# Chunked attention beside a split-float32 FFN: another order for the pieces of attention

## The chip, the cores and the metric

The kernel runs on one core of a Trainium2 chip. The metric is the device time of one execution in microseconds (us). A difference of under 0.2% (about 2 us here) can't be told from no change.

## The reference

Attention works inside chunks of 64 tokens; its output, brought to 4608 rows of 512, goes through a two-layer FFN with a squared ReLU. The weights arrive as 64-bit floats, everything else as float32.

```python
scores = scale * np.matmul(q_c, k_c.transpose(0, 1, 2, 4, 3))     # chunks of 64 x 64
scores = scores - np.max(scores, axis=-1, keepdims=True)
attn = np.exp(scores)
attn = attn / (np.sum(attn, axis=-1, keepdims=True) + 1e-09)
out = np.matmul(attn, v_c)
x = np.ascontiguousarray(out.transpose(0, 2, 1, 3)).reshape(B * S, H * D)
h = x @ w_in                                  # 4608 x 512 by 512 x 2048
r = np.maximum(h, 0.0)
return ((r * r) @ w_out).astype(np.float32)   # by 2048 x 512
```

## The kernel before, in words

**Split floats.** Every product is taken in three parts: each operand is a rounded high part plus a low part (`fp32r`), and high by high, high by low and low by high are summed in PSUM. A low part is always `value - high`, so it needs the high part first.

**Blocks and steps.** The 4608 rows are 36 pairs of chunks (128 rows), in 9 blocks of 4 pairs. The FFN of a block is 16 steps; a step is 12 products of 128x512 into `h` (line 616) and 12 out of `g` (line 653), the second set two steps behind the first (`LAG = 2`). Between them ACT and DVE make `g`, `gh` and `gl`.

**Attention of a block runs during the FFN of the block before it.** Blocks 0 and 1 have their own code at the start. From block 2 on (pair 8 on) a pair is worked in two *units* of four heads; units 16 to 23 are block 2's, unit 71 is the last. A unit goes through this chain:

- `begin`/`stack`, once for a pair: q and k come by DMA into `ring` tiles, DVE transposes them (line 310), ACT and DVE split them into `qst` and `kst` (lines 315, 321, 327, 331).
- `scores`: four products `sc` on PE (line 357), called S16 to S71 below; ACT and DVE add the parts (370, 375), then maximum, subtraction, exponential, sums with reciprocal (379 to 393), and on POOL the division (`norm`, line 396).
- `turn`: DVE transposes the shares in 32x32 blocks into half 0 of the tile `turned` (`turn_p`, line 406); SP sends them to DRAM (`send_p`, line 410, tile `scr`) and fetches them back in four quarters into half 1 (`fetch_p`, line 417), which makes the transpose whole.
- `split_p`: ACT makes the high part of `pst` (`high_p`, line 423), DVE the low part (`low_p`, line 426).
- `values`: four products `xt` on PE (line 437), called X16 to X71 below. PE's order is fixed, so if `low_p` is late, PE stands at X and all FFN products behind it stand too. Then `x` is put together and split into `xh` and `xl` for the next block's FFN (447 to 465).

**What sets the order.** `program()` adds every piece to a `Plan` with an engine, a guessed cost and the tokens that it reads and writes. FFN pieces are added in order; the pieces of a unit are slipped in among them at fractions of the block (`SPOTS`, `LEAD`, `slot`, `spread`). `Plan.run` plays the list with its guesses (`greedy`, `to_the_right`, `to_the_left`) and issues each engine's instructions in order of the planned start. So a guess or a token doesn't make anything wait on the chip; it moves places in the five queues. On the chip each queue is worked strictly in that order, with semaphore waits on what an instruction really reads and overwrites. SP issues all transfers of this part from one queue: q and k (line 280), v (line 305), shares (410, 417) and results (670).

Of the kernel before, what the change touches and what calls it, by code (L numbers as in the profile page):

```python
# [22 lines left out]
def kernel(  # L23
# [661 lines left out]
    class Plan:  # L685
# [4 lines left out]
        HOP = {PE: 0.27, DVE: 0.07, ACT: 0.07, POOL: 0.1, SP: 0.1}  # L690
        LATENCY = 2.8
        RATE = 1.9e5
        END = 1e4

        def __init__(self):
            self.ops = []
            self.writer = {}
            self.readers = {}
            self.rank = 0
            self.follows = {}  # L700
            self.followed = {}
            self.last_load = None

        def add(self, engine, cost, fn, reads=(), writes=(), size=0):
# [12 lines left out]
            for t in reads:  # L717
                self.readers.setdefault(t, set()).add(n)
            self.ops.append((engine, cost, fn, before - {n}, size, self.rank))
            if engine == SP and self.rank is not None:  # L720
# [8 lines left out]
        def greedy(self):  # L729
# [6 lines left out]
            for n in reversed(range(len(ops))):  # L736
                engine, cost, _, _, size, rank = ops[n]
                if size:
                    cost += size / self.RATE + self.LATENCY
# [10 lines left out]
            while open_:  # L750
# [7 lines left out]
                t, _, n = best  # L758
                engine, cost, fn, _, size, _ = ops[n]
                end = free[engine] = t + cost  # L760
                if size:
                    queue = max(queue, end) + size / self.RATE
                    end = queue + self.LATENCY
                if loads and loads[-1] == n:
# [34 lines left out]
        def to_the_right(self, start, after):  # L799
            ops = self.ops  # L800
            last = max(start[n] + ops[n][1] for n in start)
            busy = self.busy()
            right = {}
            for n in sorted(start, key=lambda n: (start[n], n), reverse=True):
                engine, cost, _, _, size, _ = ops[n]
                t = min((right[x] - self.hop(n, x) for x in after[n]), default=last)
                if size:
                    t = self.lately(busy, "queue", t - self.LATENCY, size / self.RATE)
                if n in self.followed:
                    t = min(t, right[self.followed[n]])  # L810
                right[n] = self.lately(busy, engine, t, cost)
            return right

        def to_the_left(self, right):
# [3 lines left out]
            for n in sorted(right, key=lambda n: (right[n], n)):  # L818
                engine, cost, _, before, size, _ = ops[n]
                t = max((end[x] + self.hop(x, n) for x in before), default=0.0)  # L820
                if n in self.follows:
                    t = max(t, start[self.follows[n]] + ops[self.follows[n]][1])
                start[n] = t = self.early(busy, engine, t, cost)
                end[n] = t + cost
                if size:
                    end[n] = self.early(busy, "queue", t + cost, size / self.RATE) + size / self.RATE + self.LATENCY
            return start
# [23 lines left out]
    def program():  # L851
# [230 lines left out]
        ]  # L1082
        spread(ops, spots)
        for b in range(1, len(blocks)):
            later(p, b)
# [6 lines left out]

    SPOTS = (0.0, 0.12, 0.62)
    KB = 1024
# [3 lines left out]
    def later(p, b):  # L1098
# [56 lines left out]
        def fetch_v(pair):  # L1155
            if pair < NPAIR:
                un = unit[NQ * pair]
                for c in range(2):
                    for r in range(2):
                        add(SP, 0.55, lambda c=c, r=r: un.load_v(c, r), ["late"], [("vraw", c, r)], size=128 * KB)  # L1160

# [29 lines left out]
        def scores(un):  # L1191
# [19 lines left out]
            add(DVE, 0.8, un.sums, every, [z])  # L1211
            add(POOL, 0.65, un.norm, [z], every)

        quarters = [(half, b) for half in range(2) for b in range(IH)]

        def turn(un):
            e = ("le", un.u % 2)
            every = [e] + [(*e, part, c) for part in range(2) for c in range(2)]
            scr = ("scr", un.u % 2)
            add(DVE, HALF, un.turn_p, every, [("ob", 0)])  # L1220
            add(SP, 0.5, un.send_p, [("ob", 0)], [scr], size=128 * KB)
            for x in quarters:
                add(SP, 0.5, lambda x=x: un.fetch_p(*x), [scr], [("ob", 1, x), *([("ob", 1)] if un.u == NQ * NN else [])], size=64 * KB)

# [23 lines left out]
        def slot(t):  # L1248
            r = []
            for at_, stages in zip(SPOTS, (((0, split_p),), ((1, scores), (1, turn), (2, begin)), ((0, values), (1, split_v)))):  # L1250
                r.append((at_, [lambda st=st, un=unit[t + on]: st(un) for on, st in stages if t + on < NU]))
# [23 lines left out]
        spots = []  # L1275
        start = 0.0
        if b == 1:
            u = NQ * NN
            spots.append((LEAD, [lambda: scores(unit[u]), lambda: turn(unit[u]), lambda: split_v(unit[u]), lambda: begin(unit[u + 1])]))
            start = LEAD + (1 - LEAD) * (1 - SPOTS[1]) / (NQ * blocks[2] + 1 - SPOTS[1])  # L1280
        if not last:
            n = NQ * blocks[b + 1]
            for i in range(n):
                spots += [(start + (1 - start) * (i + x) / n, fs) for x, fs in slot(NQ * first_pair[b + 1] + i)]
        spread(ops, spots)
# [49 lines left out]
```

## Time and profile before

| | |
|---|---|
| median of 3 runs | 934.14 us (933.08 to 934.48) |
| the profiled execution | 933.78 us, span 932.0 us |
| busy share: PE, DVE, ACT, POOL | 96%, 70%, 68%, 24% |
| granted TensorE clock, mean | 0.991 |

The span runs from the first to the last instruction that the profiler saw; the rest of the execution lies around it. A busy share is a mean over stages: what matters here are the moments in which PE stands, and what ended each of them.

### The profile page before, as it was taken

Reading aid. Unit: us, or ns where it says so; the run is one execution under the profiler, and the core shown is the slowest. Engines: PE = TensorE matmul, PEld = TensorE weight load, DVE = VectorE, ACT = ScalarE, POOL = GpSimd, SP = SyncE. Lnnn points to the kernel's source line nnn. Section 1 sums busy time; section 2 is a strip of 40 time slices with the busy share of each in tenths; the row PEclk is TensorE's granted clock in tenths of the full one; section 3 lists DMA queues with packets and bytes.
Section 4 is the critical chain, followed back from the end, with each engine's and each line's share of the span. In section 5 each row is a group of like instructions: output and inputs, shape, how many; then the busy total and the mean of one; then the engine's idle time right before and its main releaser. Section 6 shows DMA issues by size and latency. Waiting matters only on the chain.

```text
span 932.0 us, 14557 instructions
## 1 busy us (share of the span) xinstructions
PE 897.5 (96%) x4290; PEld 747.2 (80%) x4290; DVE 656.2 (70%) x1374; ACT 631.0 (68%) x1388; POOL 227.7 (24%) x354
## 2 busy tenths in 40 slices
PE   8899998689899999999999999999999999999998
PEld 7788887567778888887878888878788888888886
DVE  4999976476787787777777777767777887742111
ACT  5898857376777777767777777767777776743223
POOL 3000002133233232433242323323323333210000
PEclk9999999799999999999999999999999999999999
DMA  9896115223343334433343334333433353201001
GB/s 212 241 334 163 46 26 133 54 68 78 84 121 74 80 80 100 105 80 80 93 102 75 77 76 127 79 77 75 112 75 72 75 130 72 57 18 46 1 1 45
DMA packets 262991, 84.87 MB, mean 91 GB/s; under 512 B 212224, under 2 KB 256256, under 8 KB 262912
## 3 DMA queue, kind: packets, MB, share of 16 engines
q1 hardware_dynamic: 260800, 83.42, 36.8%
q10 hardware_dynamic: 2112, 0.52, 0.3%
q8 instruction: 34, 0.56, 0.3%
q14 instruction: 45, 0.37, 0.1%
HBM read 67.11 MB, written 16.78 MB: 90 GB/s over the span
## 4 chain that ended last, share of the span: by engine, by line
PE 77%; DVE 8%; ACT 6%; DMA 3%; issue 3%; SPq 2%; POOL 1%; DVEq 0%; POOLq 0%; ACTq 0%
PE o L653 35%; PE h L616 34%; PE xt L437 3%; PE sc L357 2%; DVE e L375 1%; PE sc L528 1%; POOL e L396 1%; DVE pst L426 1%; DMA raw<-in_moe_w_out_dram 1%; DMA v_raw<-in_v_dram 1%; ACT x L447 1%; ACT kst L327 1%; DVE x L454 1%; ACT g L627 1%; ACT e L370 1%
## 5 line engine op out<-in xcount | busy, mean ns | idle before, releaser
L616 PE MATMUL h<-xh,w 128*128 128x512 f32 x1152 | 398.2, 392 | 0.0
L653 PE MATMUL o<-w,gh 128*128 128x512 f32 x1152 | 358.7, 393 | 0.0
L653 PEld LDWEIGHTS o<-w,gh 128*128 128x128 f32 x1152 | 216.7, 189 | 46.2 <-DVE outl L665 0.2
L616 PEld LDWEIGHTS h<-xh,w 128*128 128x128 f32 x1152 | 217.5, 189 | 41.7 <-DVE w L210 0.4
L616 PE MATMUL h<-xl,w 128*128 128x512 f32 x576 | 225.8, 392 | 0.2 <-DVE xl L592 0.2
L653 PE MATMUL o<-w,gl 128*128 128x512 f32 x576 | 225.3, 391 | 0.0
L643 DVE TENSOR_TENSOR gl<-g,gh 128x512 fp32r<-128x512 f32 x144 | 103.3, 717 | 92.1 <-ACT gh L640 89.8
L627 ACT ACTIVATE g<-h 128x512 f32<-128x512 f32 x144 | 86.2, 599 | 98.6 <-DVE gl L643 46.2
L347 POOL TENSOR_TENSOR vs<-v_raw,vs 64x128 fp32r<-64x128 f32 x224 | 117.3, 524 | 127.8 <-ACT vs L342 116.9
L640 ACT CAST gh<-g 128x512 fp32r<-128x512 f32 x144 | 89.4, 621 | 71.3 <-DVE g L631 33.6
L653 PEld LDWEIGHTS o<-w,gl 128*128 128x128 f32 x576 | 108.9, 189 | 23.5
L616 PEld LDWEIGHTS h<-xl,w 128*128 128x128 f32 x576 | 108.9, 189 | 18.7 <-DVE xl L592 0.5
L375 DVE TENSOR_TENSOR e<-sc,e 64x128 f32<-64x128 f32 x224 | 64.7, 289 | 57.7 <-ACT e L370 54.8
L465 POOL TENSOR_TENSOR xl<-x,xh 128x256 fp32r<-128x256 f32 x56 | 45.4, 811 | 219.8 <-ACT xh L462 175.9
L396 POOL TENSOR_TENSOR e<-e,z 128x256 f32<-128x256 f32 x56 | 54.8, 979 | 139.2 <-DVE z L393 134.5
L454 DVE TENSOR_TENSOR x<-xt,x 64x128 f32<-64x128 f32 x224 | 64.7, 289 | 12.8 <-ACT x L447 7.5
L370 ACT COPY e<-sc 64x128 f32<-64x128 f32 x224 | 58.2, 260 | 21.1 <-PE sc L357 17.9
L327 ACT CAST kst<-ring 64x512 fp32r<-64x512 f32 x112 | 69.3, 619 | 3.8 <-DVE ring L310 1.5
L447 ACT COPY x<-xt 64x128 f32<-64x128 f32 x224 | 58.0, 259 | 9.3 <-PE xt L437 6.5
L631 DVE TENSOR_TENSOR g<-g 128x512 f32<-128x512 f32 x64 | 47.3, 739 | 23.4 <-ACT g L627 23.0
L437 PE MATMUL xt<-pst,vs 128*128 128x256 f32 x224 | 37.6, 291 | 23.9 <-DVE pst L426 23.7
L437 PEld LDWEIGHTS xt<-pst,vs 128*128 128x128 f32 x224 | 33.0, 191 | 33.9 <-issue 23.8
(71 smaller groups left out, 880.8 us busy)
## 6 DMA issues: line engine op xcount, KB each, us to landing
v_raw<-in_v_dram SPq DMA_DIRECT2D x112, 128.0 KB, 3.2
turned<-scr SPq DMA_DIRECT2D x224, 64.0 KB, 2.0
raw<-in_moe_w_in_dram SPq DMA_DIRECT2D x16, 512.0 KB, 6.8
raw<-in_moe_w_out_dram SPq DMA_DIRECT2D x16, 512.0 KB, 7.7
scr<-turned SPq DMA_DIRECT2D x56, 128.0 KB, 1.7
ring<-in_q_dram SPq DMA_DIRECT2D x216, 32.0 KB, 2.1
ring<-in_k_dram SPq DMA_DIRECT2D x216, 32.0 KB, 2.2
out_dram<-outh SPq DMA_DIRECT2D x18, 256.0 KB, 2.2
```

Source lines behind the costliest of these rows:

```text
L327: nc.scalar.copy(late["k"][other[c][half], 0, c], pairs[self.pair]["t", 1][own])
L347: nc.gpsimd.tensor_tensor(self.v[:, c][dst], self.raw_v(c)[dst], self.v.bitcast(F32)[:, c][dst], op=ALU.subtract)
L370: nc.scalar.copy(self.e[r, 2 * part:2 * part + 2], self.done[part][r, :, 1, c])
L375: nc.vector.tensor_tensor(e, self.done[part][r, :, 0, c], e, op=ALU.add)
L437: nc.tensor.matmul(self.xt[hp][:, c].rearrange("p w b a i -> p (w b a i)"), self.v[:, c, hp].rearrange("p a d -> p (a d)"), late["p"][:, : ...
L447: nc.scalar.copy(self.x[r, hp].rearrange("p c (b i) -> p c b i", b=IH), self.xt[hp][r, :, 1, :, h2])
L454: nc.vector.tensor_tensor(x, self.xt[hp][r, :, 0, :, h2], x, op=ALU.add)
L616: nc.tensor.matmul(self.h[:, :self.n], a[:, c], bb[:, c % HP, :self.n], start=c == 0 and i == 0, stop=c == NCC - 1 and i == 2,)
L627: nc.scalar.activation(self.g, self.h[:, :self.n], AF.Relu)
L640: nc.scalar.copy(self.gh[:, :self.n], self.g)
L643: nc.vector.tensor_tensor(self.gl[:, :self.n], self.g, self.gh.bitcast(F32)[:, :self.n], op=ALU.subtract)
L653: nc.tensor.matmul(acc[b, j], a[:, j * P:(j + 1) * P], bb, start=f == 0 and i == 0, stop=f == NF - 1 and i == 2,)
```

## The change

Eleven numbers and two tokens of the planner's input change; no instruction is added, removed or made larger.

```diff
-        LATENCY = 2.8
...
+            self.latency = 2.8
...
         spread(ops, spots)
+        p.latency = 1.5
         for b in range(1, len(blocks)):
             later(p, b)
...
-    SPOTS = (0.0, 0.12, 0.62)
+    SPOTS = (0.0, 0.1, 0.66)
+    SPOTS1 = (0.0, 0.15, 0.8)
...
-                        add(SP, 0.55, lambda c=c, r=r: un.load_v(c, r), ["late"], [("vraw", c, r)], size=128 * KB)
+                        add(SP, 0.65, lambda c=c, r=r: un.load_v(c, r), ["late"], [("vraw", c, r)], size=128 * KB)
...
-            add(POOL, 0.65, un.norm, [z], every)
+            add(POOL, 1.0, un.norm, [z], every)
...
-            add(DVE, HALF, un.turn_p, every, [("ob", 0)])
-            add(SP, 0.5, un.send_p, [("ob", 0)], [scr], size=128 * KB)
+            add(DVE, HALF, un.turn_p, [*every, ("pst", 1)], [("ob", 0)])
+            add(SP, 0.4, un.send_p, [("ob", 0)], [scr, *([("ob", 1)] if un.u == NQ * NN else [])], size=128 * KB)
             for x in quarters:
-                add(SP, 0.5, lambda x=x: un.fetch_p(*x), [scr], [("ob", 1, x), *([("ob", 1)] if un.u == NQ * NN else [])], size=64 * KB)
+                add(SP, 0.5, lambda x=x: un.fetch_p(*x), [scr], [("ob", 1, x)], size=64 * KB)
...
-            for at_, stages in zip(SPOTS, (((0, split_p),), ((1, scores), (1, turn), (2, begin)), ((0, values), (1, split_v)))):
+            for at_, stages in zip(SPOTS1 if b == 1 else SPOTS, (((0, split_p),), ((1, scores), (1, turn), (2, begin)), ((0, values), (1, split_v)))):
...
-        start = 0.0
+        start, end = 0.0, 1.0
         if b == 1:
...
-            start = LEAD + (1 - LEAD) * (1 - SPOTS[1]) / (NQ * blocks[2] + 1 - SPOTS[1])
+            start, end = 0.2, 0.975
...
-                spots += [(start + (1 - start) * (i + x) / n, fs) for x, fs in slot(NQ * first_pair[b + 1] + i)]
+                spots += [(start + (end - start) * (i + x) / n, fs) for x, fs in slot(NQ * first_pair[b + 1] + i)]
```

`LATENCY`, what the plan allows from the end of a transfer's issue and bytes to its landing, is now kept with each operation. In unit 16 (`un.u == NQ * NN`) each of the four fetches wrote the token `("ob", 1)`, so the plan put each behind the landing of the one before; now only the send writes it. `turn_p` reads `("pst", 1)`, the token that `low_p` of the unit before writes. `start` for block 2 goes from 0.207 to 0.2 of block 1's FFN and `end` from 1 to 0.975.

The next two lists are SP's queue from the send of unit 16's shares on (`scr_1545` before, `scr_1567` after), before and after:

```order
L410 DMA scr_1545<-turned 128x256
L670 DMA out_dram<-outl_1466 128x512
L305 DMA v_raw_0_1562<-in_v_dram 64x8x64 x2
L305 DMA v_raw_1_1576<-in_v_dram 64x8x64 x2
L417 DMA turned<-scr_1545 32x4x128
L280 DMA ring_1326<-in_q_dram 32x8x32 x6
L417 DMA turned<-scr_1545 32x4x128
L280 DMA ring_1326<-in_q_dram 32x8x32 x2
L410 DMA scr_1647<-turned 128x256
L280 DMA ring_1324<-in_k_dram 32x8x32 x2
L417 DMA turned<-scr_1545 32x4x128
L280 DMA ring_1324<-in_k_dram 32x8x32 x6
```

```order
L670 DMA out_dram<-outl_1466 128x512 x2
L305 DMA v_raw_0_1540<-in_v_dram 64x8x64 x2
L410 DMA scr_1567<-turned 128x256
L280 DMA ring_1326<-in_q_dram 32x8x32 x4
L417 DMA turned<-scr_1567 32x4x128 x4
L280 DMA ring_1326<-in_q_dram 32x8x32 x4
L280 DMA ring_1324<-in_k_dram 32x8x32 x5
L410 DMA scr_1674<-turned 128x256
L280 DMA ring_1324<-in_k_dram 32x8x32 x3
```

Before, five more issues (four of v) stand between the send and the first fetch, and 16 loads and the next send between the first fetch and the fourth, which follows the last row. After, the four fetches stand together behind four loads.

DVE in the same place: from the maximum of unit 17 (`e_1595` before, `e_1592` after) to `pst`, which is the low part of unit 16:

```order
L379 TENSOR_REDUCE m_1614<-e_1595 128x4
L382 TENSOR_TENSOR e_1595<-e_1595,m_1614 128x256
L391 TENSOR_REDUCE z_1630<-e_1595 128x4
L392 TENSOR_SCALAR z_1630<-z_1630 128x4
L393 RECIPROCAL z_1630<-z_1630 128x4
L321 TENSOR_TENSOR qst<-ring_1324,qst 64x8x64
L406 STREAM_TRANSPOSE turned<-e_1595 128x256
L321 TENSOR_TENSOR qst<-ring_1324,qst 64x8x64
L331 TENSOR_TENSOR kst<-ring_1325,kst 64x512 x2
L643 TENSOR_TENSOR gl_3_1653<-g_3_1583,gh_3_1652 128x512
L310 STREAM_TRANSPOSE ring_1325<-ring_1326 128x512
L310 STREAM_TRANSPOSE ring_1326<-ring_1324 128x512
```

```order
L379 TENSOR_REDUCE m_1611<-e_1592 128x4
L382 TENSOR_TENSOR e_1592<-e_1592,m_1611 128x256
L321 TENSOR_TENSOR qst<-ring_1324,qst 64x8x64 x2
L391 TENSOR_REDUCE z_1638<-e_1592 128x4
L392 TENSOR_SCALAR z_1638<-z_1638 128x4
L393 RECIPROCAL z_1638<-z_1638 128x4
L331 TENSOR_TENSOR kst<-ring_1325,kst 64x512
L426 TENSOR_TENSOR pst<-turned,pst 128x512
L331 TENSOR_TENSOR kst<-ring_1325,kst 64x512
L406 STREAM_TRANSPOSE turned<-e_1592 128x256
```

Before, `pst` is the row behind the last one shown, behind the turn of unit 17 and two transposes of later q and k; after, it is ahead of the turn and of those transposes.

The same engine in the middle of the kernel, from the subtraction of unit 38 (`e_4439`, `e_4434`) on; `pst` is the low part of unit 37:

```order
L382 TENSOR_TENSOR e_4439<-e_4439,m_4456 128x256
L391 TENSOR_REDUCE z_4466<-e_4439 128x4
L392 TENSOR_SCALAR z_4466<-z_4466 128x4
L393 RECIPROCAL z_4466<-z_4466 128x4
L643 TENSOR_TENSOR gl_9_4426<-g_9_4414,gh_9_4425 128x512
L406 STREAM_TRANSPOSE turned<-e_4439 128x256
L426 TENSOR_TENSOR pst<-turned,pst 128x512
```

```order
L382 TENSOR_TENSOR e_4434<-e_4434,m_4457 128x256
L426 TENSOR_TENSOR pst<-turned,pst 128x512
L391 TENSOR_REDUCE z_4471<-e_4434 128x4
L392 TENSOR_SCALAR z_4471<-z_4471 128x4
L393 RECIPROCAL z_4471<-z_4471 128x4
L631 TENSOR_TENSOR g_10_4469<-g_10_4469 128x512
L406 STREAM_TRANSPOSE turned<-e_4434 128x256
```

The low part goes from behind the turn to ahead of the sums. On the whole, `pst` stands behind the next unit's turn for 10 of the 56 units before (16, 19, 21, 23, 25, 37, 41, 53, 57, 67) and for none after.

On PE only the places of S and X among the FFN's products move. Counted in the order: from S to X of one unit there are 54 to 63 products in units 16 to 23 before and 60 to 63 after, and 72 before and 75 after from unit 25 on. X16 stands behind the 465th product before and the 468th after, X25 behind the 825th in both.

## Rows read from the trace of the kernel before

**Rows 1.** The page: its head; one stretch by engine (busy us, instructions, clock, DMA).

```profile
span 932.0 us, 14557 instructions
...
292.00:840.00 548.00, 543.28 (x2549) 452.76 (x2548) 414.27 (x945) 394.62 (x948) 171.14 (x266) 1.00 0.36 83
```

**Rows 2.** Waits from 146 to 292 us and from 292 to 832 us: total, times, longest.

```profile
PE xt L437 <- DVE pst L426: 19.1, 7, 10.3
...
PE xt L437 <- DVE pst L426: 4.6, 5, 1.0
```

**Rows 3.** Timeline of PE: X16, S18, X18, X25, two S a unit apart, X37, X70.

```profile
170.79 1.20 PE L437 MATMUL xt<-pst,vs 128*128 128x256 f32 x4 [10.29 <-DVE pst L426]
177.22 0.64 PE L357 MATMUL sc<-kst,qst 128*128 128x256 f32 x4
194.36 0.71 PE L437 MATMUL xt<-pst,vs 128*128 128x256 f32 x4 [1.81 <-DVE pst L426]
278.55 0.71 PE L437 MATMUL xt<-pst,vs 128*128 128x256 f32 x4 [1.58 <-DVE pst L426]
296.45 0.64 PE L357 MATMUL sc<-kst,qst 128*128 128x256 f32 x4
308.33 0.64 PE L357 MATMUL sc<-kst,qst 128*128 128x256 f32 x4
422.76 0.71 PE L437 MATMUL xt<-pst,vs 128*128 128x256 f32 x4 [1.01 <-DVE pst L426]
820.07 0.64 PE L437 MATMUL xt<-pst,vs 128*128 128x256 f32 x4
```

**Rows 4.** Timelines of DVE and ACT: turn 16; high and low 16; low 17, turn 18.

```profile
151.61 0.45 DVE L406 STREAM_TRANSPOSE turned<-e 128x256 f32<-128x256 f32 x1
169.31 0.62 ACT L423 CAST pst<-turned 128x512 fp32r<-128x512 f32 x1 [6.15 <-DMA turned<-scr]
169.96 0.69 DVE L426 TENSOR_TENSOR pst<-turned,pst 128x512 fp32r<-128x512 f32 x1
181.64 0.69 DVE L426 TENSOR_TENSOR pst<-turned,pst 128x512 fp32r<-128x512 f32 x1
182.84 0.45 DVE L406 STREAM_TRANSPOSE turned<-e 128x256 f32<-128x256 f32 x1 [0.51 <-POOL e L396]
```

**Rows 5.** Timeline of SP's queue: unit 16's send, first and fourth fetch; unit 18's.

```profile
152.08 0.33 SPq L410 DMA_DIRECT2D scr<-turned  x1
157.20 0.57 SPq L417 DMA_DIRECT2D turned<-scr  x1
167.14 0.45 SPq L417 DMA_DIRECT2D turned<-scr  x1
183.31 0.34 SPq L410 DMA_DIRECT2D scr<-turned  x1
185.09 1.74 SPq L417 DMA_DIRECT2D turned<-scr  x4
```

**Rows 6.** DMA issues (count, KB, median us to landing); landing of the shares from 190 to 203 us.

```profile
v_raw<-in_v_dram SPq DMA_DIRECT2D x112, 128.0 KB, 3.2
turned<-scr SPq DMA_DIRECT2D x224, 64.0 KB, 2.0
...
DMA to landing us min/median/max: 1.7/3.2/3.5
```

**Rows 7.** Stretches by engine, as in Rows 1: just behind X16, X18 and X19.

```profile
170.70:174.90 4.20, 4.11 (x12) 3.51 (x13) 1.85 (x5) 2.54 (x8) 0.63 (x1) 0.54 0.45 96
194.90:198.30 3.40, 3.40 (x11) 2.64 (x10) 3.23 (x7) 2.52 (x8) 1.41 (x2) 0.53 0.38 80
208.70:212.10 3.40, 3.40 (x10) 2.69 (x9) 1.85 (x5) 2.38 (x7) 1.37 (x3) 0.51 0.40 83
```

**Rows 8.** Timeline of DVE at X37: turn 38, low part of 37.

```profile
421.60 0.45 DVE L406 STREAM_TRANSPOSE turned<-e 128x256 f32<-128x256 f32 x1 [0.51 <-POOL e L396]
421.97 0.65 DVE L426 TENSOR_TENSOR pst<-turned,pst 128x512 fp32r<-128x512 f32 x1
```

More of the change, by code (lines that the diff above doesn't have):

```diff
@@ L718, in add @@
                 self.readers.setdefault(t, set()).add(n)
-            self.ops.append((engine, cost, fn, before - {n}, size, self.rank))
+            self.ops.append((engine, cost, fn, before - {n}, size, self.rank, self.latency))
             if engine == SP and self.rank is not None:
@@ L736, in greedy @@
             for n in reversed(range(len(ops))):
-                engine, cost, _, _, size, rank = ops[n]
+                engine, cost, _, _, size, rank, latency = ops[n]
                 if size:
-                    cost += size / self.RATE + self.LATENCY
+                    cost += size / self.RATE + latency
                 due[n] = min((due[x] - self.hop(n, x) for x in after[n]), default=self.END) - cost
@@ L758, in greedy @@
                 t, _, n = best
-                engine, cost, fn, _, size, _ = ops[n]
+                engine, cost, fn, _, size, _, latency = ops[n]
                 end = free[engine] = t + cost
@@ L762, in greedy @@
                     queue = max(queue, end) + size / self.RATE
-                    end = queue + self.LATENCY
+                    end = queue + latency
                 if loads and loads[-1] == n:
@@ L804, in to_the_right @@
             for n in sorted(start, key=lambda n: (start[n], n), reverse=True):
-                engine, cost, _, _, size, _ = ops[n]
+                engine, cost, _, _, size, _, latency = ops[n]
                 t = min((right[x] - self.hop(n, x) for x in after[n]), default=last)
                 if size:
-                    t = self.lately(busy, "queue", t - self.LATENCY, size / self.RATE)
+                    t = self.lately(busy, "queue", t - latency, size / self.RATE)
                 if n in self.followed:
@@ L818, in to_the_left @@
             for n in sorted(right, key=lambda n: (right[n], n)):
-                engine, cost, _, before, size, _ = ops[n]
+                engine, cost, _, before, size, _, latency = ops[n]
                 t = max((end[x] + self.hop(x, n) for x in before), default=0.0)
@@ L825, in to_the_left @@
                 if size:
-                    end[n] = self.early(busy, "queue", t + cost, size / self.RATE) + size / self.RATE + self.LATENCY
+                    end[n] = self.early(busy, "queue", t + cost, size / self.RATE) + size / self.RATE + latency
             return start
```

## The prediction

> **What bounds the kernel now.** I read the busy time by stretch first: from 292 to 840 us PE is busy for 543.28 of 548 us at the full clock [rows 1]. The middle is PE's own work; only its idle moments and its slow stretches can be won. The list of waits says what ends the idle moments: the products `xt` (X) wait for the low part of `pst`, seven times from 146 to 292 us, 19.1 us with one of 10.3, and five times later, 4.6 us [rows 2]. No other wait of PE there is worth a term.
>
> The timeline of PE gives the cost with what hangs on the waits. In the middle one unit lasts 308.33 - 296.45 = 11.88 us [rows 3]: 48 products at some 0.227 us, S and X at about 0.5 each. From X25 (278.55) to X70 (820.07) stand 45 units, 534.6 us at that pace; they took 541.5 [rows 3]. So **the middle has 6.9 us** to give. From X16 (170.79) to X25 there are 360 products and nine S and nine X, about 81.6 + 9.2 = 90.8 us; they took 107.8 [rows 3]. So there are **17.0 us here**, and 10.3 in the wait before X16.
>
> Part of the 17.0 is the clock. In three stretches, behind X16, X18 and X19, the granted clock was 0.54, 0.53 and 0.51 of full speed, which is the lower level of 1.2 GHz, each after PE had stood [rows 7]. They last 4.2, 3.4 and 3.4 us, so they cost 1.9 + 1.6 + 1.7 = 5.2 us. The six labelled waits behind X16 are 19.1 - 10.3 = 8.8 us [rows 2]. The other 3.0 us are smaller delays around the waits that have no label.
>
> **The change, part by part.** Nothing is added or taken away, so every cost is one of place.
>
> *The fetches of unit 16.* Its shares are turned at 151.61 [rows 4] and sent at 152.08; the first fetch is issued at 157.20, the fourth at 167.14 [rows 5]. ACT stood 6.15 us for it, the high part started at 169.31, the low part at 169.96 [rows 4], X16 at 170.79. In the new queue the four fetches stand together behind four loads. Unit 18 shows what that is worth: turn 182.84 [rows 4], send 183.31, four fetches from 185.09 in 1.74 us [rows 5], landing 2.0 us after an issue [rows 6]: the data are there about 188.4, **5.6 us after the turn starts**. Four loads fit into the time in which the first fetch waits for the send anyway (183.31 to 185.09). In the new order DVE copies one more result and transposes q ahead of unit 16's parts, and squares and transposes k before the turn: four pieces of about 0.7 us, some of them in a wait that was there before. I take turn 16 at 153.2 instead of 151.61 and the data at 158.8 instead of 169.3. Then they are not last.
>
> What is late next is DVE itself, whose list up to the low part of 16 now has S17's parts, the maximum, two low parts of q, the sums and one low part of k. Without q and k this took from S18 at 177.22 to 181.64 + 0.69 = 182.33, 5.1 us [rows 3, 4]. Three pieces of about 0.69 are added, of which I let 0.5 fill the wait for the exponential: 6.7 us. S17 stands 36 products behind S16 (which is where it was, 146.4), at 155.0; the low part ends at 161.7 and X16 starts at 161.8 to 162. PE arrives 24 products after S17, at 160.9. So about 1.1 us of the wait of 10.29 stays. X16 comes at 162.0, with three more products behind it: **8.8 us earlier**, and 0.7 more by the three products. Bounds: if everything but the fetch is hidden, 9.9; if the turn comes 4 us later than I take it, as it would if the v loads that now stand ahead of the send wait for POOL, 5.
>
> *Low part ahead of the turn.* At X37 DVE first waits 0.51 us for POOL, turns unit 38's shares (421.60), and only then makes the low part of 37 at 421.97 [rows 8]; PE waits 1.01 us for it and starts at 422.76 [rows 3]. The lists show this at X16, 19, 21, 23, 25, 37, 41, 53, 57 and 67; the timeline of PE has a wait at each, and only X18 and X20 wait without it. In the new order no turn stands there. From unit 24 on the low part is ahead even of the sums (about 0.8 us) in most units and X stands three products (0.7 us) later. So the middle should run at its pace: **-6.7 us** of the 6.9. Can the moved turn be late instead? It closes a loop: turn, data after 5.6 us, high part 0.62, low part 0.69 [rows 4], sums 0.8, 1.2 us from their end (181.64, where the next row starts) to the turn (182.84) [rows 4], and one square of 0.7: 9.7 us, against 11.88 for a unit. It is hidden with 2.2 us to spare. (The 0.8 and 0.7 are the plan's figures; its 0.69 for a low part is what the row shows.)
>
> *Block 2.* Here a unit has only 37 products on average (X16 to X23, 468 to 729 in the order): 8.5 + 1.0 = 9.5 us, against the same loop of 9.7. There is no cover left, so I expect waits of a few tenths to 1 us where q and k are split in between: about 1.0 at X18, 0.3 each at X21 and X22, and 1.0 in all at scores that now follow X by 12 products (3.3 us) instead of 18. That is 2.5 us instead of 8.8 + 3.0. None is as long as those of 1.8 us and more after which the clock fell, and waits of 1.01 us passed without a fall [rows 3], so I take the 5.2 us as won. Together 17.0 - 2.5 = **-14.5 us**. Bounds: all of 17.0, if nothing waits; 3.5, if the waits stay and the clock still falls once for 1.7.
>
> The other edits (guesses for v, send and `norm`, the spots) act through these orders; the lists up to S16 are the same but for neighbours.
>
> **Sum.** Against the profiled execution's own 933.8 us (0.4 below the median of 934.14): 933.8 - 8.8 - 0.7 - 14.5 - 6.7 = 903.1. I give one microsecond back for delays that I don't see: **904 us**.
>
> **Rivals.** *A: the fetches land later.* Shares that followed six loads of k landed after 3.2 us in the middle and 3.5 at most, not 2.0 [rows 6]. In block 2 that makes the loop 9.7 + 1.3 = 11.0 us against 9.5: seven units wait 1.5 us, 10.5 instead of the 2.5, and the clock falls once for 1.7. 904 + 8 + 1.7 = **914 us**. For it: in the new order each block of fetches follows up to four loads, and in unit 18 a load of v of 128 KB, which takes 3.2 us [rows 6], where before the fetches came first. Against it: over all 224 fetches the median is 2.0, though by the order most followed loads too. The Trainium skill (*DMA: Bandwidth & Descriptors*, section *Queues, rings and completion order*) speaks for A: a transfer's completion signal is ordered behind every earlier write of the same DMA engine, so fetches behind loads land no sooner than these. By that rule the new neighbours delay every unit and A is the result; the trace bears it out for one place of those that I looked at.
>
> *B: half of X16's wait stays*, because the send stands behind loads of v that wait for POOL: 5 us more and a slow stretch of 1.9: **911 us**. Against it: POOL is idle for most of that time.
>
> *C: slower.* The turn now waits for the low part, the low part for the data, the data for the turn before. If this loop lasted longer than a unit of the middle, every unit would be late. Its point is 11.88 us, 2.2 above the 9.7. To eat the 30 us won, 47 units must lose 0.64 each, a loop of 12.5; with fetches at the 3.5 us of the slowest row it is 11.2. At 13 us the time is 904 + 47 x 1.1 = **956 us**.
>
> *D: the order changes nothing*, since X16 hangs on something else in the same queue: 930 to 934. The 6.15 us that ACT stood for the fetch speak against it.
>
> **How the numbers follow.** Forecast 0.62, with its own range of 900.5 to 909 (899.3 would be all the bounds won, 933.8 - 9.9 - 0.7 - 17.0 - 6.9); A 0.2; B 0.12; C 0.04; D 0.02. The range from 900.5 to 914 leaves out C, D and the worse half of A. 0.2% is 1.9 us: faster 0.95, same 0.01, slower 0.04.
>
> **What would show it.** X16 at 161 to 163 us with a wait near 1 us; fetches of unit 16 in one row of four; X25 near 254 us; no wait of X for `pst` behind 260 us and 11.88 us from S to S; a full clock behind X18 and X19. Wrong if X18 to X23 wait 1.5 us each (A), if the send of unit 16 comes behind 155 us (B), or if S to S is above 12 us in the middle (C).

## The result and the profile after

The changed kernel takes 903.98 us (median of four runs, 903.73 to 904.32) beside 934.31 us of the kernel before on the same chip (933.08 to 935.25): a ratio of 0.9676, 95% interval 0.966 to 0.9693, that is 30 us less. The forecast was 904. Its profiled execution is the one of 903.73 us. The size is right nearly term by term; what the terms come from is not as I said, and that is the larger part of what follows.

From the page and from single views of the kernel after: the head of the page, the middle by engine (columns as in [rows 1]), and what X waited for from 146 to 292 us. Behind 292 us that view has no line for X any more.

```profile
span 901.9 us, 14559 instructions
...
292.00:840.00 548.00, 548.00 (x2572) 459.13 (x2572) 402.58 (x914) 393.88 (x923) 163.74 (x254) 1.00 0.35 82
...
PE xt L437 <- DVE pst L426: 3.2, 5, 1.1
```

In the timeline of PE of the kernel after these rows are X16, S18, X18, X21, S25, S26, X25 and X70, to be read beside [rows 3]:

```profile
162.13 0.71 PE L437 MATMUL xt<-pst,vs 128*128 128x256 f32 x4 [0.88 <-DVE pst L426]
165.43 0.64 PE L357 MATMUL sc<-kst,qst 128*128 128x256 f32 x4
182.46 0.71 PE L437 MATMUL xt<-pst,vs 128*128 128x256 f32 x4 [1.08 <-DVE pst L426]
212.14 0.71 PE L437 MATMUL xt<-pst,vs 128*128 128x256 f32 x4 [0.89 <-DVE pst L426]
237.32 0.64 PE L357 MATMUL sc<-kst,qst 128*128 128x256 f32 x4
249.20 0.64 PE L357 MATMUL sc<-kst,qst 128*128 128x256 f32 x4
255.82 0.64 PE L437 MATMUL xt<-pst,vs 128*128 128x256 f32 x4
790.41 0.64 PE L437 MATMUL xt<-pst,vs 128*128 128x256 f32 x4
```

And these are the turn of unit 16 on DVE, its send and its four fetches in SP's queue and its low part on DVE, beside [rows 4, 5]:

```profile
152.99 0.41 DVE L406 STREAM_TRANSPOSE turned<-e 128x256 f32<-128x256 f32 x1
153.43 0.33 SPq L410 DMA_DIRECT2D scr<-turned  x1
156.46 1.73 SPq L417 DMA_DIRECT2D turned<-scr  x4
161.31 0.68 DVE L426 TENSOR_TENSOR pst<-turned,pst 128x512 fp32r<-128x512 f32 x1
```

The reader is to see three things. PE is busy for all 548.00 us of the middle, where it was for 543.28. X16 starts at 162.13 instead of 170.79. And no wait of X is longer than 1.1 us; from 146 to 840 us the granted clock is full in every stretch.

| term | forecast | measured, from the rows |
| --- | --- | --- |
| to X16 | -8.8 | 162.13 - 170.79 = -8.66 |
| X16 to X25 | -0.7 - 14.5 = -15.2 | (255.82 - 162.13) - (278.55 - 170.79) = -14.07 |
| X25 to X70 | -6.7 | (790.41 - 255.82) - (820.07 - 278.55) = -6.93 |
| the rest | +1 given back | 903.73 - 933.78 + 29.66 = -0.39 |

### The profile page after: what moved, and what is told of

It reads as the page before. It is cut to its first block, busy times and chain, and to the rows that moved or that the text cites. A ratio compares the mean times of both kernels' runs of the same rounds, so it can differ in the third digit from the quotient of the medians.

```text
span 901.9 us, 14559 instructions
## 1 busy us (share of the span) xinstructions
PE 890.3 (99%) x4290; PEld 746.1 (83%) x4290; DVE 657.2 (73%) x1374; ACT 638.3 (71%) x1388; POOL 228.7 (25%) x354
## 4 chain that ended last, share of the span: by engine, by line
PE 93%; DVE 3%; ACT 1%; issue 1%; SPq 1%; DMA 1%; POOL 0%; DVEq 0%; POOLq 0%; ACTq 0%
PE h L616 42%; PE o L653 42%; PE xt L437 3%; PE sc L357 3%; PE sc L528 1%; PE xt L579 1%; DVE e L375 1%; PE warm_ps L866 0%; DVE qst L321 0%; PE k L504 0%; DVE pst L426 0%; PE q L504 0%; DMA qk_raw<-in_q_dram 0%; DVE e L382 0%; ACT e L370 0%
## 5 line engine op out<-in xcount | busy, mean ns | idle before, releaser
L347 POOL TENSOR_TENSOR vs<-v_raw,vs 64x128 fp32r<-64x128 f32 x224 | 121.2, 541 | 155.3 <-ACT vs L342 125.7
L465 POOL TENSOR_TENSOR xl<-x,xh 128x256 fp32r<-128x256 f32 x56 | 43.5, 777 | 125.8 <-ACT xh L462 90.8
L631 DVE TENSOR_TENSOR g<-g 128x512 f32<-128x512 f32 x64 | 44.6, 697 | 19.3 <-ACT g L627 18.7
L633 ACT ACTIVATE g<-g 128x512 f32<-128x512 f32 x80 | 50.6, 632 | 2.3
L423 ACT CAST pst<-turned 128x512 fp32r<-128x512 f32 x56 | 34.7, 619 | 19.0 <-DMA turned<-scr 18.5
```

Of the source, the lines that this page charges most:

```text
L347: nc.gpsimd.tensor_tensor(self.v[:, c][dst], self.raw_v(c)[dst], self.v.bitcast(F32)[:, c][dst], op=ALU.subtract)
```

## The experiments

Twelve kernels ran in three groups, each group beside the kernel before on its own chip. First all of them together; the ratio is to the kernel before of the same group. A difference of times between two rows can be one between two chips; the intervals of the ratios tell whether it is clear.

One more thing limits what a small difference says. Up to S16 PE has the same 794 matmuls in the same order in all fourteen profiled executions, and yet S16 starts anywhere from 146.25 to 148.38 us. With X 18 products behind S all five queues hold the order of the kernel after up to 138 us, and S16 is still 1.5 us later (147.97, after 146.50). So I say below what part of a small difference lies ahead of S16.

| kernel | us | ratio, 95% interval |
| --- | --- | --- |
| after | 903.98 | 0.9676, 0.966 to 0.9693 |
| before + fetches of 16 together | 925.5 | 0.9894, 0.9875 to 0.9914 |
| before + low part ahead of the turn | 928.78 | 0.9929, 0.9909 to 0.9949 |
| before + both | 919.85 | 0.9835, 0.9812 to 0.9859 |
| before + new places | 925.67 | 0.9917, 0.9893 to 0.9941 |
| after, fetches of 16 chained | 911.52 | 0.9749, 0.9724 to 0.9773 |
| after, turn free of the low part | 909.17 | 0.9729, 0.9716 to 0.9742 |
| after, old places | 908.2 | 0.9725, 0.9706 to 0.9744 |
| after, all old guesses | 922.87 | 0.9886, 0.9865 to 0.9907 |
| after, old guess for a landing | 925.75 | 0.9914, 0.9899 to 0.9929 |
| after, X 18 products behind S | 906.32 | 0.9707, 0.9688 to 0.9727 |
| after, X 27 products behind S | 907.1 | 0.9714, 0.9695 to 0.9733 |
| after, eight fetches a unit | 981.74 | 1.0507, 1.0492 to 1.0523 |

### One edit at a time on the kernel before

The theory that the prediction stands for: the two edits of order (fetches of unit 16 together; low part ahead of the next turn) carry the gain. The rival: the new places do, which put more feed-forward products between S of one unit and X of the unit ahead of it.

*Fetches together:*

```diff
-            add(SP, 0.5, un.send_p, [("ob", 0)], [scr], size=128 * KB)
+            add(SP, 0.5, un.send_p, [("ob", 0)], [scr, *([("ob", 1)] if un.u == NQ * NN else [])], size=128 * KB)
...
-                add(SP, 0.5, lambda x=x: un.fetch_p(*x), [scr], [("ob", 1, x), *([("ob", 1)] if un.u == NQ * NN else [])], size=64 * KB)
+                add(SP, 0.5, lambda x=x: un.fetch_p(*x), [scr], [("ob", 1, x)], size=64 * KB)
```

> The kernel before with one edit: the four fetches of unit 16 no longer follow one another in the plan, so they stand in one block in SP's queue. The low part of 16 still stands behind turn 17, and the spots and guesses are those of before. My theory (the fetch that came last held the high part, and the slow clock came from the wait): the data of unit 16 are there about 158 to 160 us, X16 starts near 162 to 164 instead of 170.8, and the slow stretch behind X16 goes: 934.3 - 8 - 1.9 = 924 us (922 to 928). The middle stays as before, 541 us from X25 to X70. Rival one (the wider distance from S to X is what brings X16 forward, not the fetches): the wait moves to the low part or to the exponential, X16 comes no more than 2 us earlier, 931 or more.

Measured 925.5 us. X16 in the timeline of PE of this kernel:

```profile
164.73 0.71 PE L437 MATMUL xt<-pst,vs 128*128 128x256 f32 x4 [2.25 <-DVE pst L426]
```

The wait before X16 falls from 10.29 to 2.25 us, X16 starts 16.4 us behind S16 instead of 24.4, and no slow stretch follows X16: this step of the prediction holds by itself.

*Low part ahead of the turn:*

```diff
-            add(DVE, HALF, un.turn_p, every, [("ob", 0)])
+            add(DVE, HALF, un.turn_p, [*every, ("pst", 1)], [("ob", 0)])
```

> The kernel before with one edit: a unit's low part stands ahead of the next unit's turn. The fetches of unit 16 stay chained, the spots and guesses are those of before. My theory (X waits where the low part stands behind a turn): X16 still waits about 10 us; the waits of X behind it in block 2 fall from 8.8 us to under 3 and the two slow stretches behind X18 and X19 go (3.3 us); the middle loses the waits at X25, X37, X41, X53, X57 and X67, so X25 to X70 comes near 536 instead of 541.5. 934.3 - 6 - 3.3 - 5.5 = 919.5 us (917 to 924). Rival one (the wider distance from S to X is what counts, 75 products instead of 72): waits of about the old lengths stay because the low part itself is late by the loop, 929 or more.

Measured 928.78 us, nine us worse than expected. The list of waits of this kernel, 146 to 292 us and 292 to 832 us:

```profile
PE xt L437 <- DVE pst L426: 18.8, 8, 9.2
...
PE xt L437 <- DVE pst L426: 2.3, 6, 0.7
```

Without the 9.2 of X16 there are 9.6 us of waits left in block 2, where there were 8.8 [rows 2]. No turn stands ahead of a low part in this kernel, and X18 to X23 wait 0.9 to 1.8 us all the same. So the turn was not what the low part stood behind for long. In the middle, from X25 to X70, the edit brings 1.9 us (539.66 instead of 541.52) of the forecast's 6.7. And it has a cost: before, 14 low parts of the middle stood ahead of the next unit's sums, and in this kernel none does.

*Both:*

> The kernel before with both edits of order (fetches of unit 16 in one block, low part ahead of the next turn), its spots and guesses kept. My theory says that these two carry nearly all: 934.3 minus the sum of what each brings alone, 910 us (906 to 913), X25 to X70 at 535 to 537, X16 at 162 to 163. Rival one (spots and guesses carry it): 920 or more, with waits of X for the low part left in the middle.

Measured 919.85 us, ten us worse than expected: the two gains add up (9.5 + 6.3 = 15.8 against the 935.03 us of the kernel before on that chip, measured 15.2), and half of the 30 us is missing.

*New places alone* (24 products from the next unit's S to X in block 2 instead of 18 to 21, 27 in the middle instead of 24):

```diff
-    SPOTS = (0.0, 0.12, 0.62)
+    SPOTS = (0.0, 0.1, 0.66)
+    SPOTS1 = (0.0, 0.15, 0.8)
...
-            start = LEAD + (1 - LEAD) * (1 - SPOTS[1]) / (NQ * blocks[2] + 1 - SPOTS[1])
+            start, end = 0.2, 0.975
```

> The kernel before with the new places alone: SPOTS, SPOTS1, start and end. The fetches of unit 16 stay chained, the low part may stand behind the next unit's turn, the guesses are those of before. Between the scores of one unit and the values product of the unit ahead of it stand 24 products of the feed-forward in block 2 instead of 18, and 27 in the middle instead of 24. My theory has changed after the first four runs: in block 2 the low part stands on the vector engine behind the maximum and the sums of the next unit's scores, some 5 to 6 us behind their start, and 18 products with those scores last 4.7 us; the distance is what removes the wait. By it f4 keeps a wait of 4 to 6 us at X16 with one slow stretch, has waits under 1 us at X18 to X23 and none in the middle: 934.3 - 5 - 9 - 5 = 915 us (912 to 920). The step of my prediction (the low part's place ahead of the turn is what counts): 926 or more, with waits of 1 to 2 us left in block 2.

Measured 925.67 us, 10.7 worse than my changed theory said, with 10.2 us at X16. The places bring 7.6 us by themselves (933.3 - 925.67), most of them behind X16 in block 2: from X16 to X25 it takes 98.85 us, where before took 107.76 and after takes 93.69. The middle takes 540.40 us, 1.1 less than before. So the rival does not carry the 30 us either.

### One edit undone in the kernel after

*Fetches chained again* (the first diff, backwards):

> The kernel after with one edit undone: the fetches of unit 16 follow one another in the plan again and are spread over some eight loads in SP's queue. My theory: X16 waits about 8 to 10 us again and starts near 170, with one slow stretch behind it; all behind X25 is as in the kernel after, 534.6 us from X25 to X70: 904 + 8.8 + 1.9 = 914.7 us (911 to 917). Rival one (the wider distance is what brought X16 forward): 904 to 906.

Measured 911.52 us: X16 waits 4.29 us and starts at 167.88, with the clock at 1.2 GHz behind it. Inside the range, but the wait is less than half of the old one, and 1.9 of the 7.5 us lie ahead of S16 (148.38). In SP's queue the fourth fetch now starts 5.75 us behind the first (158.57 to 164.32), where it was 9.94 before [rows 5]. The low part ahead of the turn does not do that alone, nor do the places (9.4 and 10.9 us in those two kernels). In the plan each chained fetch stands behind the guessed landing of the one before, and that guess is now 1.3 us shorter; this is the likely reason, but no run parts it from the other guesses.

*All guesses of before:*

```diff
-        p.latency = 1.5
+        p.latency = 2.8
...
-                        add(SP, 0.65, lambda c=c, r=r: un.load_v(c, r), ["late"], [("vraw", c, r)], size=128 * KB)
+                        add(SP, 0.55, lambda c=c, r=r: un.load_v(c, r), ["late"], [("vraw", c, r)], size=128 * KB)
...
-            add(POOL, 1.0, un.norm, [z], every)
+            add(POOL, 0.65, un.norm, [z], every)
...
-            add(SP, 0.4, un.send_p, ...
+            add(SP, 0.5, un.send_p, ...
```

> The kernel after with the guesses of before (2.8 us for a landing, 0.55 for a load of v, 0.5 for a send, 0.65 for the normalisation); both edits of order and the new places are kept. If places and order carry the gain: 903.5 to 907, with the 534.6 us from X25 to X70 and a wait near 1 us at X16. Rival (the guesses carry part of it, through the lists of the load queue and the vector engine): 909 or more.

Measured 922.87 us. This is the run that overturned my account: S, X and the products stand on PE as in after, both edits of order and all places are kept, and 19 us are gone. X16 to X23 wait 1.5 to 1.9 us each.

*One number of these, the guess for a landing:*

```diff
-        p.latency = 1.5
+        p.latency = 2.8
```

> The kernel after with one number undone: the plan's guess for the time from the end of a transfer's bytes to its landing is 2.8 us again instead of 1.5; the other guesses, both edits of order and the places are those of after. On PE the program is the same. On the vector engine nearly every low part of block 2, and most of the middle, stands behind the next unit's sums instead of ahead of them. My theory after eight runs: this number is what most of the gain hangs on. With 2.8 the low part comes some 6 to 7 us behind the start of the next scores, PE after 24 x 0.227 + 0.64 = 6.1 us, so X waits 1 to 2 us at each unit of block 2 and a few tenths in every second unit of the middle: 919 to 925, as with all the old guesses (922.9). The step of my prediction, in which the guesses cost and bring nothing of their own beside the two edits of order and the places: 904 to 907.

Measured 925.75 us: putting back this one number costs 21.8 of the 30 us. The profiled executions lie 24.3 us apart: 1.1 us of that lie ahead of S16, 1.6 between S16 and X16, 15.5 between X16 and X25 (109.15 instead of 93.69) and 6.2 between X25 and X70. In block 2 all eight X wait, and behind three of them (X16, X17, X21) the clock falls; the first line is the list of waits from 146 to 292 us. The other lines are from the timelines of SP, ACT, DVE and PE and show unit 20: the send and the fetches, the high part, the sums of unit 21, the low parts of q and k, the low part of 20, S21 and X20.

```profile
PE xt L437 <- DVE pst L426: 14.7, 8, 2.4
...
202.17 0.34 SPq L410 DMA_DIRECT2D scr<-turned  x1
205.65 1.81 SPq L417 DMA_DIRECT2D turned<-scr  x4
...
211.94 0.62 ACT L423 CAST pst<-turned 128x512 fp32r<-128x512 f32 x1
...
210.02 0.42 DVE L391 TENSOR_REDUCE z<-e 128x4 f32<-128x256 f32 x1 [0.48 <-ACT e L387]
...
210.88 1.71 DVE L321 TENSOR_TENSOR qst<-ring,qst 64x512 fp32r<-64x512 f32 x2
212.62 0.68 DVE L331 TENSOR_TENSOR kst<-ring,kst 64x512 fp32r<-64x512 f32 x1
213.23 0.68 DVE L426 TENSOR_TENSOR pst<-turned,pst 128x512 fp32r<-128x512 f32 x1
...
205.91 0.64 PE L357 MATMUL sc<-kst,qst 128*128 128x256 f32 x4
214.05 0.71 PE L437 MATMUL xt<-pst,vs 128*128 128x256 f32 x4 [2.04 <-DVE pst L426]
```

The same unit in the kernel after, fetches, high part, low part, sums of unit 21, X20:

```profile
194.69 1.81 SPq L417 DMA_DIRECT2D turned<-scr  x4
...
198.97 0.62 ACT L423 CAST pst<-turned 128x512 fp32r<-128x512 f32 x1
...
200.41 0.69 DVE L426 TENSOR_TENSOR pst<-turned,pst 128x512 fp32r<-128x512 f32 x1
201.02 0.41 DVE L391 TENSOR_REDUCE z<-e 128x4 f32<-128x256 f32 x1
...
201.77 0.64 PE L437 MATMUL xt<-pst,vs 128*128 128x256 f32 x4
```

From the first fetch to the high part it takes 6.29 us with the guess of 2.8 and 4.28 with 1.5. In the first case ACT waits for no shares anywhere from 146 to 292 us; they have landed (median 2.0 us behind an issue), and ACT and DVE do q, k and the sums before they turn to them. In the second ACT waits for shares five times, 2.7 us in all: its list comes to them when they land. By the lists of DVE the low part stands ahead of the next unit's sums in all 47 units behind block 2 with 1.5, and in none with 2.8. In block 2 it stands ahead of them in three of eight units (17, 20 and 23) with 1.5, again in none with 2.8; of the other five, four have one or two pieces of q, k or the feed-forward fewer ahead of the low part, and unit 18 has as many. Counted from the start of the next S, the low parts of block 2 start after 4.58 to 6.36 us with 1.5 and after 6.65 to 7.63 us with 2.8; PE is at X after about 6.1 (24 products of 0.227 and 0.64 for S). From X25 to X70 the kernel with 2.8 takes 540.78 us, with 1.5 it takes 534.59; no turn stands ahead of a low part in either.

Why 1.5 is nearer to the chip: the plan lets a fetch land its issue (0.5) + 64 KB at 190 GB/s (0.34) + the guess behind the start of its issue, 3.64 us with 2.8 and 2.34 with 1.5; the rows show 2.0 [rows 6].

*Places of before:*

```diff
-    SPOTS = (0.0, 0.1, 0.66)
-    SPOTS1 = (0.0, 0.15, 0.8)
+    SPOTS = (0.0, 0.12, 0.62)
...
-            start, end = 0.2, 0.975
+            start, end = LEAD + (1 - LEAD) * (1 - SPOTS[1]) / (NQ * blocks[2] + 1 - SPOTS[1]), 1.0
```

> The kernel after with the places of before (SPOTS, no SPOTS1, start and end): 18 to 21 products from the next unit's scores to X in block 2, 24 in the middle. Both edits of order and the new guesses are kept. If the guess for a landing is what counts, the low part is ready some 3.7 us behind the scores in the middle, where PE comes after 24 x 0.227 + 0.64 = 6.1 us: no wait there, 534.6 us from X25 to X70; in block 2 waits of about 1 us as in the kernel with SPOTS1 at 0.15 and 0.65 (906.3): 905 to 910. If the places carry their own part in the middle: 912 or more, with waits of X behind 292 us.

Measured 908.2 us. The middle of this kernel and, below it, of the one with the guess of 2.8, by engine:

```profile
292.00:840.00 548.00, 548.00 (x2574) 459.15 (x2573) 402.97 (x922) 394.96 (x929) 160.57 (x255) 1.00 0.35 82
```

```profile
292.00:840.00 548.00, 544.99 (x2550) 452.88 (x2549) 428.64 (x939) 391.98 (x945) 176.18 (x264) 1.00 0.35 82
```

With the old places PE does not wait in the middle at all; with the old guess it does. So the three products more are worth nothing there. Of the 4.2 us (908.2 - 903.98, and as much in the profiled executions) 1.7 lie ahead of S16 and 2.3 between S16 and X25, where the longest waits are 1.77 and 1.43 us; whether the first figure has to do with the places, the runs don't tell. Beside both edits of order, but with the old guesses, the same places cost time: ratios of 0.9835 without them and 0.9886 with them, intervals apart. On the kernel before, without any of the other edits, they brought 7.6 us.

*Turn free of the low part:*

```diff
-            add(DVE, HALF, un.turn_p, [*every, ("pst", 1)], [("ob", 0)])
+            add(DVE, HALF, un.turn_p, every, [("ob", 0)])
```

> The kernel after without the dependency that sets a low part ahead of the next turn; everything else is kept. The plan then puts only the low parts of units 16 and 21 behind a turn. If the guess for a landing already brings the low part forward, this edit is worth the two places, 0.4 to 0.9 us each: 904.5 to 907. The step of my prediction (this edit takes the middle's 6.7 us): 910 or more, though the list shows no turn ahead of a low part there.

Measured 909.17 us, 5.2 more (4.7 in the profiled executions, 4.4 of it ahead of S24 and 0.4 ahead of S16): PE is busy for all of the middle here too. Turn 17 stands ahead of the low part of 16 once more and first waits for POOL, as in [rows 8]; the first line is the high part of 16 on ACT:

```profile
162.08 0.62 ACT L423 CAST pst<-turned 128x512 fp32r<-128x512 f32 x1 [0.88 <-DMA turned<-scr]
...
162.34 0.45 DVE L406 STREAM_TRANSPOSE turned<-e 128x256 f32<-128x256 f32 x1 [0.51 <-POOL e L396]
162.73 0.69 DVE L426 TENSOR_TENSOR pst<-turned,pst 128x512 fp32r<-128x512 f32 x1
```

X16 waits 1.87 us instead of 0.88, and behind it the clock falls to 1.2 GHz (0.59 granted from 163.8 to 166.8), which I had not put into the expectation. It looks like the mechanism of the prediction, but the turn is not what the low part waits for: the high part ends at 162.08 + 0.62 = 162.70 and the low part starts at 162.73. The high part stood 0.88 us for shares that landed at 162.05, where in after they landed at 159.66, since the edit also moved SP's list (the send starts at 154.74 instead of 153.43, the first fetch at 158.68 instead of 156.46). At X21, the other place where the turn is ahead, the wait is 0.80 us instead of 0.89. So the run gives the step of the prediction no support.

### How far X stands behind S in block 2

```diff
-    SPOTS1 = (0.0, 0.15, 0.8)
+    SPOTS1 = (0.0, 0.15, 0.65)
```

> The kernel after with SPOTS1 at 0.15 and 0.65: in block 2 a values product stands 18 to 21 products behind the next unit's scores instead of 24. The low part still stands ahead of every turn, and the fetches of unit 16 together. By the distance theory the low part comes 5 us behind the start of those scores and is ready about 5.7 us behind it, where PE arrives after 18 x 0.227 + 0.64 = 4.7 us: waits of 0.7 to 1.3 us at each unit with 18, some 5 us in all, 907 to 911. Rival (the low part's place ahead of the turn is enough in block 2): 903.5 to 905.5.

Measured 906.32 us; of the six X with 18 products X16, X18, X20 and X22 wait 1.78, 1.42, 1.53 and 0.55 us, X21 and X23 not; of the two with 21 X19 waits 0.18. The places are as expected. The size is under it and not clear: the interval of the ratio overlaps that of after, and 1.5 us of the profiled difference lie ahead of S16.

```diff
-    SPOTS1 = (0.0, 0.15, 0.8)
+    SPOTS1 = (0.0, 0.12, 0.85)
```

> The kernel after with SPOTS1 at 0.12 and 0.85: in block 2 a values product stands 27 products behind the next unit's scores instead of 24, and the scores behind it follow after 9 to 12 instead of 12 to 15. By the distance theory the waits left at X18, X21, X22 and X23 (1.08, 0.89, 0.18, 0.21 us) go, since 0.7 us more of cover stands there: 901.5 to 903. Rival (the scores that now follow at 9 products wait for the q and k that are split there, or the low parts of q and k are what is late): 903.5 to 907.

Measured 907.1 us. The waits of X18 to X23 do fall, from 2.36 to 0.76 us in all. But the plan now issues the fetches of unit 16 at 160.15 instead of 156.46, X16 waits 2.60 us, and the clock falls behind it. Each move of a place moves the lists of all queues, so this pair tells the distance's worth only at X18 to X23.

### The loop through the fetches

Each unit's four fetches are cut into eight; bytes and places stay.

```diff
-            nc.sync.dma_start(
-                out=late["t"][r:r + 32, 1].rearrange("p (g n) -> p g n", g=2 * IH),
-                in_=self.scr.rearrange("(g j) b n -> j b g n", j=32)[:, b],
-            )
+            for lo, hi in ((0, 2), (2, 4)):
+                nc.sync.dma_start(
+                    out=late["t"][r:r + 32, 1].rearrange("p (g n) -> p g n", g=2 * IH)[:, lo:hi],
+                    in_=self.scr.rearrange("(g j) b n -> j b g n", j=32)[:, b, lo:hi],
+                )
```

> The kernel after with each unit's four fetches cut into eight issues of half the size: same bytes, same places. An issue takes about 0.45 us of the load queue, so the last shares of a unit land 1.8 us later. By the loop of my prediction (9.7 us + 1.8 = 11.5, under the 11.88 of a unit in the middle) the middle loses nothing and block 2 some 1 to 2 us at each of seven units: 911 to 917, X25 to X70 still 534.6 us. By what the trace of after shows in the middle (in every second unit the high part waits for the shares, and the low part of unit 37 ends 1.1 us before its X starts), 0.7 us are lost in some 20 units too: 925 to 935. If shares are not last anywhere: 904 to 906.

Measured 981.74 us, beyond every expectation. Of this kernel: the eight fetches of unit 35 in SP's queue, its high part on ACT, X35 on PE, the high part of 36 and two low parts 30 units apart (36 and 66); and what DVE sat idle for ahead of its low parts from 292 to 840 us.

```profile
393.02 3.68 SPq L418 DMA_DIRECT2D turned<-scr  x8
...
398.21 0.62 ACT L424 CAST pst<-turned 128x512 fp32r<-128x512 f32 x1 [4.56 <-DMA turned<-scr]
...
399.70 0.71 PE L438 MATMUL xt<-pst,vs 128*128 128x256 f32 x4 [1.66 <-DVE pst L427]
...
408.68 0.62 ACT L424 CAST pst<-turned 128x512 fp32r<-128x512 f32 x1 [1.47 <-DMA turned<-scr]
409.33 0.69 DVE L427 TENSOR_TENSOR pst<-turned,pst 128x512 fp32r<-128x512 f32 x1 [1.16 <-DMA ring<-in_q_dram]
815.89 0.69 DVE L427 TENSOR_TENSOR pst<-turned,pst 128x512 fp32r<-128x512 f32 x1 [2.63 <-DMA ring<-in_q_dram]
...
  ACT pst L424: 47.8, 22
  DMA ring<-in_q_dram: 18.6, 11
  DMA ring<-in_k_dram: 8.6, 3
```

The same in the kernel after at unit 37, which has q and k beside it as 35 has: its four fetches, high part and X37, then the low parts of 36, 37 and 38 and of 66, and the turns of 37 and 38:

```profile
391.16 1.82 SPq L417 DMA_DIRECT2D turned<-scr  x4
...
395.94 0.62 ACT L423 CAST pst<-turned 128x512 fp32r<-128x512 f32 x1 [1.87 <-DMA turned<-scr]
...
398.38 0.64 PE L437 MATMUL xt<-pst,vs 128*128 128x256 f32 x4
...
382.90 0.68 DVE L426 TENSOR_TENSOR pst<-turned,pst 128x512 fp32r<-128x512 f32 x1
388.23 0.44 DVE L406 STREAM_TRANSPOSE turned<-e 128x256 f32<-128x256 f32 x1
396.60 0.69 DVE L426 TENSOR_TENSOR pst<-turned,pst 128x512 fp32r<-128x512 f32 x1 [0.65 <-ACT pst L423]
399.12 0.45 DVE L406 STREAM_TRANSPOSE turned<-e 128x256 f32<-128x256 f32 x1 [0.51 <-POOL e L396]
406.66 0.69 DVE L426 TENSOR_TENSOR pst<-turned,pst 128x512 fp32r<-128x512 f32 x1
740.13 0.69 DVE L426 TENSOR_TENSOR pst<-turned,pst 128x512 fp32r<-128x512 f32 x1
```

Thirty units last 815.89 - 409.33 = 406.56 us, 13.55 each, where they lasted 740.13 - 382.90 = 357.23, 11.91 each: 1.64 us more a unit for 1.86 us more of issue (3.68 - 1.82). The clock also falls in six of these fifteen pairs of units; the nine others take 26.87 us each, 1.53 more a unit. So there are a few tenths of a us of cover in the middle, not the 2.2 of the prediction.

The list puts 47.8 us of DVE's idle time down to the high part and 27.2 us to loads of q and k. The second label does not hold: in all 37 of these waits the low part starts 0.03 us behind the end of its own high part (unit 36: 408.68 + 0.62 = 409.30, then 409.33), and 13 of the 14 loads that the list names landed only 0.2 to 0.6 us behind that start. Where a high part had waited, it starts at most 0.31 us behind the landing of its unit's last share. So the shares set these low parts back, not the loads behind them in the queue.

## Why the prediction came out, and where its reasons failed

**The fetch of unit 16** held. Turn 16 starts at 152.99 (forecast 153.2), the low part ends at 161.99 (161.7), X16 starts at 162.13 (162.0), and with this edit alone the wait falls to 2.25 us. The four loads did not fit into the wait for the send, as I had them: the first fetch comes 3.03 us behind it and not 1.78, and the data land at 159.66 and not 158.8, but DVE is last even so.

**"Low part ahead of the turn", -6.7 us in the middle and most of block 2's -14.5**: the size was right, the step fails. I read from the two orders that no turn stands ahead of a low part any more and gave that the credit. With that edit alone block 2 keeps its waits and the middle wins 1.9 us, and without it the middle loses nothing. What carries the gain in the middle is that the low part stands ahead of the next unit's **sums**, which I named in half a sentence ("ahead even of the sums"); in block 2 it stands ahead of them in three units of eight and otherwise mostly with fewer other pieces ahead of it. What puts it there is the guess for a landing, which stands in no term of mine; I had the guesses "act through these orders" and never asked which guess sets which order. Of the 6.93 us won in the middle, 6.19 (540.78 - 534.59) are gone when that number is put back, and all of the 14.07 of block 2. The forecast was right because it supposed the order of the whole changed kernel and that nearly no X waits in it, whatever made that order; that the total came out says nothing for the step.

**Block 2, 2.5 us of waits left**: measured 1.08 at X18 (forecast 1.0), 0.89 at X21 and 0.18 at X22 (0.3 each), 0.21 at X23 (0) and none at the scores (1.0). X16 to X25 took 93.69 us, 1.1 more than forecast; those 1.1 have no label in the list of waits. The **clock** stayed full from 146 to 840 us, as I took it to.

**The loop of 9.7 us, 2.2 to spare**: wrong (and its terms add up to 9.6). The formula took unit 18, ahead of whose turn no q and k are split and whose fetches were issued 1.78 us behind the send [rows 5]; at unit 37 of the kernel after it is 2.5. In the rows above, from the low part of 36 to that of 37 it is 5.33 us to the turn + 7.71 to the high part + 0.66 = 13.70, and the next unit takes 10.06. Only the pair fits into its 23.76 us, which is PE's own pace for two units; that little of it is spare is not seen in these rows but in the run with eight fetches. Rival C did not occur, but its point is nearer than I put it: 1.86 us of issue more a unit turn 30 us of gain into 47 of loss (981.74 - 934.24).

**Rival A** (shares land later behind loads) did not come about: from 146 to 292 us their median is 2.1 us and the longest 3.6, and ACT waits 2.7 us for them in all, under cover. By the rule of the Trainium skill that I cited (*DMA: Bandwidth & Descriptors*, *Queues, rings and completion order*) they land no sooner than the loads ahead of them. The trace of after agrees, in that none of its 224 fetches landed ahead of a transfer issued before it, but this cost next to nothing: of the 13 fetches that took over 3 us to land, two landed within 0.4 us behind a load issued ahead of them. Of the other eleven, five had no load under way when they were issued, and six landed at least 1.7 us behind the last such load. **B**: the send came at 153.43, ahead of its 155. **D** is excluded by the result.

What stays open: what the guess for a landing brings by itself, since it was only undone and never put alone into the kernel before; the edits undone one at a time cost 21.8, 7.5, 5.2 and 4.2 us, more than the 30 together, so they do not simply add up. Open, too, is how the three other guesses and the start and end of block 2 share what is left (all old guesses 922.87, the one 925.75).

## What to carry to other kernels

Where a planner makes the order, its guesses are part of the program: compare each with the measured row first (here a landing of 3.64 us planned against 2.0 measured), for putting one such number back cost 21.8 of 30 us. Judge an edit by undoing it alone and by doing it alone: the same places brought 7.6 us to the kernel before, cost some 3 beside the edits of order with the old guesses, and bring at most 4 with the new ones. When a view puts a wait down to a transfer, look whether the transfer had landed by then and what ended just before. And take the spare time of a loop from its longest unit, queue by queue, not from the one that is easiest to read.

## What the runs showed of the hardware

The clock behind a wait of X. I took every wait of X of at least 1.2 us from 100 to 850 us in the profiles of before, after and the twelve experiments, and read the mean granted clock from 0.2 to 3.2 us behind the start of that X.

| wait before X | how many | of these at under 0.95 behind it |
| --- | --- | --- |
| 1.25 to 1.78 us | 30 | 0 |
| 1.80 to 3.02 us | 35 | 19 |
| 3.74 to 10.29 us | 5 | 5 |

Between 1.8 and 3 us it goes either way (2.25 us without a fall in one kernel, 2.29 with one in another): behind waits shorter than the forecast's 1.8 us no fall was seen, and behind longer ones, up to 3 us, about every second time. The kernel before shows both: a fall behind X19's 1.94 us and none behind X23's 2.00.
